# Transposing q and k on TensorE in place of DMA transposes, in an attention kernel with a gated MLP behind it

## Chip, cores and metric

The kernel runs on one core of a Trainium2 chip. The metric is the device time of one execution in microseconds; the time before is the median of 3 runs.

## What is computed

Eight batch entries, twelve heads, 448 positions, head dimension 64. q and k are normalised by their root mean square and scaled by g_q and g_k; then softmax attention; the heads are joined to rows of 768, and each entry goes through a gated MLP with a spatial mixing matrix.

```python
q_n, k_n = (rmsnorm(q, g_q), rmsnorm(k, g_k))        # x / sqrt(mean(x*x) + 1e-6) * g
scores = scale * np.matmul(q_n, k_n.transpose(0, 1, 3, 2))
attn = softmax(scores)
x = np.matmul(attn, v)  # heads joined: (8, 448, 768)
...
h = np.maximum(x @ w_in, 0.0)                        # w_in: 768 x 1024
u, v = h[..., :512], h[..., 512:]
v_n = (v - mu) / np.sqrt(var + 1e-06)
v_s = np.einsum('ts,bsd->btd', w_spatial, v_n) + b_spatial[None, :, None]
out = (u * v_s) @ w_out                              # w_out: 512 x 768
```

## The kernel before

**Tiling.** Positions lie as 112 partitions x 4 chunks (p c). The twelve heads of an entry are taken in three groups G of four heads (heads g, g+3, g+6, g+9); eight entries make 24 groups. Inside a group the heads form two pairs pr; a pair's two heads lie on the two halves of 128 partitions after a transpose. A *step* t is one score tile: one pair and two of the four chunks of keys, so a group is four steps, n = t % 4, and there are 96 steps and three more that drain.

**A group's way.** load (L70, SP's queue) brings q and k as float32. squares (L148, POOL) and reduce (L155, DVE) give the sums of squares; rstd (L162 and L163, ACT) gives 1/rms as Exp(-0.5 Ln); scaled (L168, POOL) multiplies into the bf16 tiles n0 and n1. Then q and k are turned so that the head dimension lies on partitions: for group 0 by transposes (L185, eight TensorE transposes into one PSUM buffer for a pair, evicted by DVE in L190 and L191, k with the gains g2_col), for all other groups by transpose_dma (L197, two DMA transposes on SP's queue, k into the tile kr) and k_scale (L205, DVE, from kr to kT). scores (L217) makes four matmuls of 64 x 112 by 64 x 448 into the PSUM tile pss (four banks), expo (L228, ACT) takes the exponential to bf16. Of the group before, sums (L238) adds the exponentials up, recip (L246 and L247, ACT) takes the reciprocal, values (L257) multiplies with v, and xt_store (L265, DVE) writes the product to xt.

**The MLP of an entry** is cut in units that fill PE between score tiles: unit_v (L283) with its relu (L275 on DVE, L273 on ACT), stats, ln_rstd and ln_apply (L289 to L303) for the LayerNorm, unit_u (L312), unit_s (L322) with the gating product (L325, DVE), and unit_o (L336) with its eviction (L341 on DVE, L339 on ACT) and the store (L345, SP's queue). s = (t - 15) % 12 says which units a step has: 0 to 2 unit_v, 3 to 5 unit_u, 6 and 7 unit_s, 8 to 11 unit_o. The units of an entry start four steps after its last score tile, so they run beside the next entry's scores; the last entry's run alone at the end.

**The order.** The scheduling is manual: each engine executes its instructions in the order in which the program's loop issues them. Within a step that order is: scores and expo, loads, the preparation of later groups (squares of group G+3 at n = 2 and 3; reduce at n = 3 and 0; rstd, scaled and transpose_dma of group G+2 at n = 1; k_scale of group G+1 at n = 0), the LayerNorm pieces, sums or values of group G-1, and then the MLP units. For groups 0 to 2 (t < 12) scores and expo go in halves of two matmuls and half an exponential, and groups 1 and 2 have preparation steps of their own at t = 0 to 6.

**Buffers.** All PSUM tiles other than pss come from one ring of four banks (ps_w), each taken again four allocations later: transposes, sums, values and all MLP units share it. n0 and n1 have two buffers each, qT, kT and kr three, the raw q and k tiles four.

```python
        if n == 1 and 3 <= T < NGT:      # T = G + 2
            rstd(T)
            scaled(T, 0)
            scaled(T, 1)
            transpose_dma(T, 0)
            transpose_dma(T, 1)
        if n == 0 and 3 <= K < NGT:      # K = G + 1
            k_scale(K)
```

Of the kernel before, what the change touches and what calls it, by code (L numbers as in the profile page):

```python
# [10 lines left out]
BF = mybir.dt.bfloat16  # L11
AF = mybir.ActivationFunctionType
ALU = mybir.AluOpType
# [5 lines left out]
def kernel(  # L19
# [17 lines left out]
    P = 112  # L37
    NC = 4
# [3 lines left out]
    pe, act, dve, pool, sync = nc.tensor, nc.scalar, nc.vector, nc.gpsimd, nc.sync  # L42
# [9 lines left out]
    qt_pool = ctx.enter_context(tc.tile_pool(name="qt", bufs=3))  # L52
# [13 lines left out]
    def load(G, i, l0=0, nl=4):  # L66
        b, g = divmod(G, NG)
        if (G, i) not in raw:
            raw[G, i] = qk_pool.tile([P, 4, NC * D], FP, name="qf" if i == 0 else "kf")
        sync.dma_start(out=raw[G, i][:, l0:l0 + nl], in_=(q_g, k_g)[i][b][g][:, l0:l0 + nl])  # L70

    def load_v(b):
        t = v_pool.tile([P, H, NC, D], BF, name="vt")
        pool.dma_start(  # L74
            out=t.rearrange("p h c d -> p h (c d)"),
            in_=v[b].rearrange("h (p c) d -> p h (c d)", c=NC))
        vb[b] = t
# [29 lines left out]
    for t in vn_t:  # L107
# [4 lines left out]
    g2_col = const.tile([128, 1], FP)  # L112
    dve.scalar_tensor_tensor(out=g2_row, in0=g_row[:, 0].rearrange("o t d -> o (t d)"), scalar=scale,
                             in1=g_row[:, 1].rearrange("o t d -> o (t d)"),
                             op0=ALU.mult, op1=ALU.mult)
# [3 lines left out]
    def load_w_in():  # L119
        for l in range(4):  # L120
            pool.dma_start(  # L121
                out=w_in[32 * l:32 * l + 32, :, :],
                in_=moe_w_in[192 * l:192 * l + 192, :].rearrange("(j p) f -> p j f", p=32))
# [16 lines left out]
    sqt, sqs, rst, nrm, qkt = {}, {}, {}, {}, {}  # L140
# [34 lines left out]
    def qk_tiles(G):  # L175
        if G not in qkt:
            qkt[G] = (qt_pool.tile([128, NC, 2, P], BF, name="qT"),
                      qt_pool.tile([128, NC, 2, P], BF, name="kT"))
        return qkt[G]

    def transposes(G, pr):
        ps = ps_w.tile([128, 8, 128], BF, name="ps")
        for i in range(2):
            for c in range(NC):
                pe.matmul(out=ps[:, 4 * i + c, 0:P],  # L185
                          lhsT=nrm[G, i][:, c, 2 * pr:2 * pr + 2, :],
                          rhs=ident[0:P, 0:P], is_transpose=True,
                          start=(i == 0 and c == 0), stop=(i == 1 and c == NC - 1))
        qT, kT = qk_tiles(G)
        dve.tensor_copy(out=qT[:, :, pr, :], in_=ps[:, 0:4, 0:P])  # L190
        dve.tensor_scalar(out=kT[:, :, pr, :], in0=ps[:, 4:8, 0:P], scalar1=g2_col, scalar2=None,  # L191
                          op0=ALU.mult)

    def transpose_dma(G, i):
        kr = qt_pool.tile([128, NC, 2, P], BF, name="kr") if i == 1 else None
        t = qk_tiles(G)[0] if i == 0 else kr
        sync.dma_start_transpose(out=t.rearrange("q c r p -> q (c r) p"),  # L197
                                 in_=nrm[G, i].rearrange("p c l d -> p (c l d)"))
        if i == 1:
            krs[G] = kr  # L200

    krs = {}

    def k_scale(G):
        dve.tensor_scalar(out=qkt[G][1], in0=krs.pop(G), scalar1=g2_col, scalar2=None, op0=ALU.mult)  # L205


    exps, xts = {}, {}
# [2 lines left out]
    def scores(t, half=None):  # L211
        G, n = divmod(t, 4)
        pr, c0 = n // 2, 2 * (n % 2)
        qT, kT = qkt[G]
        for c in (0, 1) if half is None else (half,):
            for h in range(2):
                pe.matmul(out=pss[:, 2 * c + h, 0:S],  # L217
                          lhsT=kT[64 * h:64 * h + 64, c0 + c, pr, :],
                          rhs=qT[64 * h:64 * h + 64, :, pr, :],
                          start=True, stop=True)  # L220

    def expo(t, half=None):
        G, n = divmod(t, 4)
        pr, c0 = n // 2, 2 * (n % 2)
        if c0 == 0 and half in (None, 0):
            exps[G, pr] = e_pool.tile([P, NC * 2, S], BF, name="et")
        a, m = (0, 4) if half is None else (2 * half, 2)
        act.activation(out=exps[G, pr][:, 2 * c0 + a:2 * c0 + a + m, :], in_=pss[:, a:a + m, 0:S],  # L228
                       func=AF.Exp, bias=0.0, scale=1.0)
# [118 lines left out]
    NGT = B * NG  # L348
    NST = NGT * 4
    for pr in range(2):  # L350
        l = 2 * pr
# [22 lines left out]
    for t in range(NST + 3):  # L374
        G, n = divmod(t, 4)
        s = t - 15
        b, s = divmod(s, 12)
        moe = b >= 0 and b < B - 1
        early = G < NG


        if t < NST:
            if early:
                if t > 0:
                    scores(t, 1)
                    expo(t, 0)
                expo(t, 1)
                if t + 1 < NST:
                    scores(t + 1, 0)
            else:  # L390
                if t == 12:
                    scores(t, 1)
                    expo(t, 0)
                    expo(t, 1)
                else:
                    scores(t)
                    expo(t)


        if G + 4 < NGT and n < 2:  # L400
            load(G + 4, n)
        if n == 1 and G % NG == 0 and G // NG + 1 < B:
            load_v(G // NG + 1)
        if t == 1:
            load_w_in()
        if t == 4:
            load_w_rest()


        if t == 0:  # L410
            rstd(1)
            scaled(1, 0)
            scaled(1, 1, eng=dve)
            squares(2, 0)
        elif t == 1:
            transpose_dma(1, 0)
            transpose_dma(1, 1)
            squares(2, 1, eng=dve)
            reduce(2, 0)
            reduce(2, 1)  # L420
        elif t == 2:
            k_scale(1)
            rstd(2)
            scaled(2, 0)
        elif t == 3:
            scaled(2, 1, eng=dve)
        if t == 4:
            transpose_dma(2, 0)
            transpose_dma(2, 1)
        if t == 6:  # L430
            k_scale(2)
        A, R, T, K = G + 3, G + 2, G + 2, G + 1
        if n == 2 and A < NGT:
            squares(A, 0)
        if n == 3 and A < NGT:
            squares(A, 1)
            reduce(A, 0)
        if n == 0 and 3 <= R < NGT:
            reduce(R, 1)
        if n == 1 and 3 <= T < NGT:  # L440
            rstd(T)
            scaled(T, 0)
            scaled(T, 1)
            transpose_dma(T, 0)
            transpose_dma(T, 1)
        if n == 0 and 3 <= K < NGT:
            k_scale(K)


        if moe:  # L450
            if s == 1:
                stats(b, 0)
            elif s == 2:
                stats(b, 1)
            elif s == 3:
                stats(b, 2)
                stats(b, 3)
                ln_rstd(b)
            elif s == 4:
                ln_apply(b)  # L460


        if 0 < G <= NGT:
            if n == 0:
                sums(G - 1)
                recip(G - 1)
            elif n < 3:
                values(G - 1, n - 1)
                xt_store(G - 1, n - 1)
        if t == 15:  # L470
            dve.tensor_copy(out=w_spT[96:113, NC - 1, :, :],
                            in_=bst[96:113, :].rearrange("q (p c) -> q c p", c=NC))
        if 15 <= t < 19:
            w_sp_unit(t - 15)


        if moe:
            if s == 0:
                unit_v(b, 0, dve)
                unit_v(b, 1, dve)  # L480
            elif s == 1:
                unit_v(b, 2, dve)
            elif s == 2:
                unit_v(b, 3, dve)
            elif s == 3:
                unit_u(b, 0, act)
            elif s == 4:
                unit_u(b, 1, act)
                unit_u(b, 2, act)
            elif s == 5:  # L490
                unit_u(b, 3, dve)
            elif s == 6:
                unit_s(b, 0)
                unit_s(b, 1)
            elif s == 7:
                unit_s(b, 2)
                unit_s(b, 3)
            elif s == 8:
                unit_o(b, 0, dve)
                unit_o(b, 1, act)  # L500
                unit_o(b, 2, dve)
            elif s == 9:
                unit_o(b, 3, dve)
                unit_o(b, 4, dve)
            elif s == 10:
                unit_o(b, 5, dve)
                unit_o(b, 6, act)
            else:
                unit_o(b, 7, dve)
# [44 lines left out]
```

## Time and profile before

| what | value |
|---|---|
| median of 3 runs | 354.74 us (354.63 to 356.36) |
| the profiled execution's own time | 354.63 us |
| its span, first to last instruction | 352.8 us |
| mean granted TensorE clock | 0.991 |
| busy: PE, ACT, DVE, POOL | 288.7, 222.0, 210.6, 186.3 us |
| DMA transposes, median from issue to landing | 2.9 us (q), 3.6 us (k), 23 each |
| SP's queue waiting with a transpose for POOL's n (L197) | 132.0 us |
| packets of the hardware DMA queue q1 | 69216, 43.59 MB |

How to read it: the span and the busy times are of one profiled execution, whose time is 1.8 us over its span. PE is TensorE's matmuls, PEld its weight loads, DVE, ACT, POOL and SP the vector, scalar, GpSimd and sync engines; L185 is line 185 of the kernel before. Matmuls are pipelined, and their records overlap: four score matmuls whose record lasts 0.58 us let the next matmul start after 0.52 us. In an answer on groups, "x23 | 11.7, 507 | 18.0 <-DMA kr<-n 18.0" is the count, busy microseconds, mean nanoseconds of one, and the idle microseconds before them with what ended them. In an answer on waits the three numbers are microseconds in all, times, and the longest. A timeline row is start, duration, engine, line and operation, with the idle time before it in brackets.

### The profile page before, as it was taken

To read this page: it belongs to the slowest core of one execution; us is meant where nothing else is said; L and a number is where in the kernel's file an instruction comes from. 1 tells how busy PE (TensorE), PEld (TensorE's weight loads), DVE (VectorE), ACT (ScalarE), POOL (GpSimd) and SP (SyncE) were. 2 spreads that over 40 slices of the span, in tenths; PEclk is the share of its full clock that TensorE was granted. 3 is DMA by queue.
4 is the path that set the end of the run, shared out by engine and by line. 5 is a ranking of instruction groups with operands and counts; after the bars stand their busy time and mean duration, and the time that the engine had idled before them with its cause. 6 is when DMAs were issued, how large, how long until landed. Compare 5 with 4: busy or idle time off the path is not lost.

```text
span 352.8 us, 5856 instructions
## 1 busy us (share of the span) xinstructions
PE 288.7 (82%) x2338; PEld 134.5 (38%) x2338; DVE 210.6 (60%) x352; ACT 222.0 (63%) x273; POOL 186.3 (53%) x113
## 2 busy tenths in 40 slices
PE   0222634688999989997999989998999899999993
PEld 0111201224435433542344434443444345445552
DVE  3385304226887587757764886488648865745551
ACT  2334434375778768874876786778677867785331
POOL 7259850926746774687197549654965484000000
PEclk9999999999999999998999999999999999999998
DMA  7979999497346994899339983999299554302305
GB/s 194 245 159 167 203 187 203 89 148 156 55 110 144 209 243 106 145 213 248 101 82 215 242 170 69 220 252 166 58 223 261 62 54 111 99 2 62 96 0 158
DMA packets 81651, 52.26 MB, mean 148 GB/s; under 512 B 44271, under 2 KB 77264, under 8 KB 81624
## 3 DMA queue, kind: packets, MB, share of 16 engines
q1 hardware_dynamic: 69216, 43.59, 57.2%
q0 software_dynamic: 12400, 8.30, 16.6%
q8 instruction: 18, 0.29, 0.4%
q14 instruction: 9, 0.07, 0.1%
q10 hardware_dynamic: 8, 0.00, 0.0%
HBM read 38.58 MB, written 11.01 MB: 141 GB/s over the span
## 4 chain that ended last, share of the span: by engine, by line
issue 37%; POOL 34%; PE 18%; DMA 7%; ACT 1%; DVE 1%; ACTq 0%; POOLq 0%; DVEq 0%
POOL sqt L148 19%; POOL n L168 12%; PE ps L336 5%; DMA qT<-n 4%; PE ps L283 4%; PE ps L312 3%; PE pss L217 2%; PE ps L257 2%; PE ps L322 2%; POOL vt L74 2%; ACT et L228 1%; DMA out_dram<-osb 1%; DMA g_row<-in_g_k_dram 1%; PE ps L238 1%; POOL w_in L121 1%
## 5 line engine op out<-in xcount | busy, mean ns | idle before, releaser
L228 ACT ACTIVATE et<-pss 112x1792 bf16<-112x1792 f32 (+1 forms) x109 | 160.4, 1483 | 68.8 <-PE pss L217 67.9
L168 POOL TENSOR_TENSOR n<-qf,rs 112x1024 bf16<-112x1024 f32 (+1 forms) x25 | 48.5, 1939 | 111.3 <-ACT rs L163 109.4
L217 PE MATMUL pss<-qT,kT 64*112 64x448 bf16 x384 | 64.6, 408 | 39.9 <-ACT et L228 33.0
L155 DVE TENSOR_REDUCE ms<-sqt 112x16 f32<-112x1024 f32 (+1 forms) x50 | 58.1, 1171 | 40.4 <-POOL sqt L148 38.4
L265 DVE TENSOR_TENSOR xt<-ps,rc 128x448 bf16<-128x448 f32 x48 | 29.6, 617 | 41.2 <-PE ps L257 35.7
L217 PEld LDWEIGHTS <-kT 64*112 64x112 bf16 x384 | 22.1, 134 | 79.2 <-issue 66.8
L257 PE MATMUL ps<-et,vt 112*32 112x448 bf16 x768 | 49.6, 382 | 0.0
L336 PE MATMUL ps<-w_out,gt 128*112 128x384 bf16 x256 | 47.5, 330 | 1.7 <-DVE osb L341 1.4
L283 PE MATMUL ps<-w_in,xt 128*112 128x512 bf16 x192 | 45.8, 383 | 0.1
L148 POOL TENSOR_TENSOR sqt<-qf 112x1024 f32<-112x1024 f32 x23 | 44.4, 1932 | 0.0
L312 PE MATMUL ps<-xt,w_in 128*128 128x448 bf16 x192 | 41.3, 361 | 2.2 <-DVE vs L275 2.2
L168 POOL TENSOR_TENSOR n<-kf,rs 112x1024 bf16<-112x1024 f32 x21 | 40.0, 1906 | 0.0
L148 POOL TENSOR_TENSOR sqt<-kf 112x1024 f32<-112x1024 f32 x21 | 39.7, 1890 | 0.0
L336 PEld LDWEIGHTS <-gt 128*112 128x112 bf16 x256 | 31.3, 129 | 18.4 <-issue 11.1
L283 PEld LDWEIGHTS <-xt 128*112 128x112 bf16 x192 | 23.4, 130 | 19.4 <-issue 6.6
L341 DVE COPY osb<-ps 112x384 f32<-112x384 f32 x46 | 24.4, 553 | 7.5 <-PE ps L336 5.9
L322 PE MATMUL ps<-w_spT,vn 112*128 112x448 bf16 (+1 forms) x128 | 26.9, 353 | 0.0
L257 PEld LDWEIGHTS <-vt 112*32 112x32 bf16 x768 | 16.8, 100 | 26.4 <-issue 19.5
L312 PEld LDWEIGHTS <-w_in 128*128 128x128 bf16 x192 | 17.6, 100 | 24.2 <-issue 11.1
L238 PE MATMUL ps<-et,ones 112*32 112x448 bf16 x384 | 24.8, 382 | 0.0
L325 DVE TENSOR_TENSOR gt<-ps,us 128x448 bf16<-128x448 f32 x32 | 20.0, 625 | 6.8 <-PE ps L322 4.5
L289 DVE BATCH_NORM_STATS2 s<-vs 112x6 f32<-112x512 bf16 x32 | 21.8, 680 | 2.5 <-ACT vs L273 2.5
(47 smaller groups left out, 184.0 us busy)
## 6 DMA issues: line engine op xcount, KB each, us to landing
out_dram<-osb SPq DMA_DIRECT2D x31, 336.0 KB, 3.6
qf<-in_q_dram SPq DMA_DIRECT2D x23, 448.0 KB, 6.3
kf<-in_k_dram SPq DMA_DIRECT2D x23, 448.0 KB, 7.4
vt<-in_v_dram POOLq DMA_DIRECT2D x8, 672.0 KB, 13.0
w_in<-in_moe_w_in_dram POOLq DMA_DIRECT2D x4, 384.0 KB, 11.9
w_out<-in_moe_w_out_dram POOLq DMA_DIRECT2D x1, 768.0 KB, 13.7
qf<-in_q_dram SPq DMA_DIRECT2D x2, 224.0 KB, 3.6
kf<-in_k_dram SPq DMA_DIRECT2D x2, 224.0 KB, 3.8
```

What stands on the lines that cost most here:

```text
L148: (eng or pool).tensor_tensor(out=t[:, 0:nl, :], in0=x, in1=x, op=ALU.mult)
L155: dve.tensor_reduce(out=sqs[G][:, i, NC * l0:NC * (l0 + nl)], in_=sqt.pop((G, i, l0))[:, 0:nl, :].rearrange("p l (c d) -> p (l c) d", d=D) ...
L168: (eng or pool).tensor_tensor(out=nrm[G, i][:, :, l0:l0 + nl, :].rearrange("p c l d -> p l c d"), in0=raw[G, i][:, l0:l0 + nl, :].rearrang ...
L217: pe.matmul(out=pss[:, 2 * c + h, 0:S], lhsT=kT[64 * h:64 * h + 64, c0 + c, pr, :], rhs=qT[64 * h:64 * h + 64, :, pr, :], start=True, stop ...
L228: act.activation(out=exps[G, pr][:, 2 * c0 + a:2 * c0 + a + m, :], in_=pss[:, a:a + m, 0:S], func=AF.Exp, bias=0.0, scale=1.0)
L238: pe.matmul(out=ps[32 * l:32 * l + 32, 0:S], lhsT=ones, rhs=exps[G, l // 2][:, 2 * c + l % 2, :], start=(c == 0), stop=(c == NC - 1), tile ...
L257: pe.matmul(out=ps[32 * l:32 * l + 32, 0:S], lhsT=vb[b][:, 3 * l + g, c, 32 * half:32 * half + 32], rhs=exps[G, l // 2][:, 2 * c + l % 2, ...
L265: dve.tensor_tensor(out=xts[b][:, 2 * g + half, :], in0=pst.pop((G, half))[:, 0:S], in1=rec[G], op=ALU.mult)
L283: pe.matmul(out=ps[0:P, :], lhsT=xts[b][:, j, c * P:(c + 1) * P], rhs=w_in[:, j, DH:DF], start=(j == 0), stop=(j == 5))
L312: pe.matmul(out=ps[:, 0:S], lhsT=w_in[:, j, 128 * f:128 * f + 128], rhs=xts[b][:, j, :], start=(j == 0), stop=(j == 5))
L322: pe.matmul(out=ps[:, 0:S], lhsT=vn_t[b % 2][0:kp, c, 128 * f:128 * f + 128], rhs=w_spT[0:kp, c, :, :].rearrange("p c s -> p (c s)"), star ...
L336: pe.matmul(out=ps[0:P, 0:384], lhsT=gts[b][:, f, c * P:(c + 1) * P], rhs=w_out[:, f, r], start=(f == 0), stop=(f == 3))
```

## The change

The change was announced as "every engine's order written out by hand in steps of four score tiles, one exponential per step, filler assigned to fixed steps". What the diff holds is one thing: transpose_dma and k_scale are removed, and groups 1 to 23 use the helper transposes, as group 0 does already. The scores, the exponentials (halves for t < 12, whole ones after), sums, values and MLP units keep their places.

For groups from 3 on, the call for a group's first pair of heads stands at n = 3, two steps after its scaled, and the one for the second pair at n = 0 of the next group; both stand after the step's scores and expo and ahead of sums or values and the MLP units in program order, on PE's and on DVE's queue alike. Each call takes one of the four PSUM buffers. The tile kr goes.

```diff
-    def transpose_dma(G, i):
-        kr = qt_pool.tile([128, NC, 2, P], BF, name="kr") if i == 1 else None
-        t = qk_tiles(G)[0] if i == 0 else kr
-        sync.dma_start_transpose(out=t.rearrange("q c r p -> q (c r) p"),
-                                 in_=nrm[G, i].rearrange("p c l d -> p (c l d)"))
-        if i == 1:
-            krs[G] = kr
-
-    krs = {}
-
-    def k_scale(G):
-        dve.tensor_scalar(out=qkt[G][1], in0=krs.pop(G), scalar1=g2_col, scalar2=None, op0=ALU.mult)
...
         elif t == 1:
-            transpose_dma(1, 0)
-            transpose_dma(1, 1)
+            transposes(1, 0)
             squares(2, 1, eng=dve)
             reduce(2, 0)
             reduce(2, 1)
         elif t == 2:
-            k_scale(1)
+            transposes(1, 1)
             rstd(2)
             scaled(2, 0)
         elif t == 3:
             scaled(2, 1, eng=dve)
         if t == 4:
-            transpose_dma(2, 0)
-            transpose_dma(2, 1)
+            transposes(2, 0)
         if t == 6:
-            k_scale(2)
+            transposes(2, 1)
...
             scaled(T, 0)
             scaled(T, 1)
-            transpose_dma(T, 0)
-            transpose_dma(T, 1)
-        if n == 0 and 3 <= K < NGT:
-            k_scale(K)
+        if n in (0, 3) and 3 <= G + (2 if n == 3 else 1) < NGT:
+            transposes(G + (2 if n == 3 else 1), 0 if n == 3 else 1)
```

## Prediction

> **What bounds the kernel now.** I read the engine shares first, then a table of busy time by stretches, then the waits inside the steady part, then the timeline of one group. A step is one score tile, four steps are one group of four heads, twelve steps are one batch entry; n is the step's place in its group, s its place in the entry's gated MLP.
>
> ```profile
> PE 288.7 (82%) x2338; PEld 134.5 (38%) x2338; DVE 210.6 (60%) x352; ACT 222.0 (63%) x273; POOL 186.3 (53%) x113
> ...
> PE   0222634688999989997999989998999899999993
> ```
>
> PE leads, but the slices show two regimes: up to about slice 9 (some 80 us) it is mostly idle, then full. The stretch from 79.5 us, where the first MLP units are issued, to 322.5 us:
>
> ```profile
> 79.50:322.50 243.00, 231.36 (x1956) 107.78 (x1959) 167.13 (x285) 179.16 (x205) 140.67 (x78) 0.99 0.73 146
> ```
>
> The columns are PE, weight loads, DVE, ACT, POOL. PE is busy for 231.4 of 243 us, the next engine (ACT) for 179. PE's waits in that stretch are few:
>
> ```profile
> PE pss L217 <- ACT et L228: 6.6, 5, 1.7
> PE ps L312 <- DVE vs L275: 2.2, 1, 2.2
> PE ps L336 <- DVE osb L341: 1.4, 6, 0.2
> ```
>
> So in the steady part whatever is added to PE's queue lengthens the run, except for what fills those 10 us. The page's chain of waits is not used: it runs through POOL and "issue" because POOL idles for its turn, and it does not show that PE has no gaps.
>
> Before 80 us, ACT's exponentials and PE's score matmuls take turns, and one stall is due to the transfers that the change removes (start, duration, what ended the idle time):
>
> ```profile
> 48.85 1.72 ACT L228 ACTIVATE et<-pss 112x896 bf16<-112x896 f32 x2 [2.88 <-PE pss L217]
> ...
> 53.57 0.45 DVE L205 TENSOR_SCALAR kT<-kr,g_col 128x896 bf16<-128x896 bf16 x1 [9.17 <-DMA kr<-n]
> ...
> 54.08 1.00 PE L217 MATMUL pss<-qT,kT 64*112 64x448 bf16 x4 [5.27 <-DVE kT L205]
> ...
> 55.11 1.72 ACT L228 ACTIVATE et<-pss 112x896 bf16<-112x896 f32 x2 [4.54 <-PE pss L217]
> ```
>
> The exponentials of steps 7 and 8 start 6.26 us apart. Step 11 has the same work in its order, and the one after it starts 2.80 us later (69.43 to 72.23). The stall is 3.5 us.
>
> **What the Trainium skill says.** "TensorE: Matmul & The Clock Gate", Part 4, PE-mode transpose: about 275 ns for one transpose in a kernel, and its output lands in PSUM, so that a copy is needed; this trace has 298 ns for each of group 0's transposes, and copies behind them. It adds that a transpose does not count as work for the clock gate; I therefore leave the early part at half clock (16 sums or values take 1.69 us there and 0.94 later). Same page, Back-to-back issue gap: a stream of load and matmul pairs runs at about 81 ns each at 128 columns, an isolated gap is columns/2.4 + 2.5 ns; no row of before shows either at full clock. "VectorE: DVE Perf Modes", Why PSUM operands drop a tier: a PSUM source loses the fastest copy mode; the trace agrees, 448 elements from PSUM take 0.39 to 0.44 us and 896 from SBUF take 0.51.
>
> ```profile
> L205 DVE TENSOR_SCALAR kT<-kr,g_col 128x896 bf16<-128x896 bf16 x23 | 11.7, 507 | 18.0 <-DMA kr<-n 18.0
> ...
> L185 PE MATMUL ps<-ident,n 112*128 112x112 bf16 x16 | 1.9, 298 | 8.5 <-POOL n L168 8.5
> ...
> L191 DVE TENSOR_SCALAR kT<-ps,g_col 128x448 bf16<-128x448 bf16 x2 | 0.9, 442 | 0.0
> ...
> L190 DVE COPY qT<-ps 128x448 bf16<-128x448 bf16 x2 | 0.8, 392 | 3.9 <-PE ps L185 3.9
> ```
>
> **Removed.** 46 DMA transposes (SP, L197) and 23 k_scale (DVE, 0.51 us). The transposes' landing (2.9 and 3.6 us median) lies three steps ahead of its use, so in the steady part it costs nothing, and removing it gains nothing. SP no longer waits for n (132 us of its waits); loads and stores behind it may start earlier, but no PE wait in the steady part names a load, so I price that at 0. The early stall goes: -3.5.
>
> **Added.** 46 calls of the transposes helper, 8 transposes and two DVE evictions each. How long PE is held by one call T: at half clock the eight in group 0 start 0.09 us apart, hence 0.75 us. At full clock nothing shows it. Lower end 8 x (112/2.4+2.5) = 0.4 us. Upper end: four transposes of w_sp hold PE for 0.53 us (89.05 to 89.58), 0.10 apart, hence 0.9 us for eight; but their weights are strided and load in 199 ns each, while contiguous 128-column loads (w_in, vn) take 97 to 100. I take the page's 81 ns scaled by 112/128, 8 x 71 = **0.57 us**; the sums, 16 pairs in 0.87 us, show that PE can issue at 54 ns.
>
> **Call at n = 3 (first half of group G+2): a new wait.** It stands behind that step's scores and ahead of all MLP filler; PE is in order, so the MLP units and the next scores behind it wait too, and through them ACT's exponentials; on DVE the evictions wait for it with LayerNorm statistics, relus and output copies behind them. It needs both n tiles, which rest on a chain that begins with the scores of n = 1: exponential, Ln and Exp of rstd, two POOL multiplications.
>
> ```profile
> 220.51 0.59 PE L217 MATMUL pss<-qT,kT 64*112 64x448 bf16 x4
> ...
> 223.10 0.23 ACT L163 ACTIVATE rs<-lnms 112x32 f32<-112x32 f32 x1
> ...
> 223.41 1.90 POOL L168 TENSOR_TENSOR n<-qf,rs 112x1024 bf16<-112x1024 f32 x1 [3.29 <-ACT rs L163]
> ...
> 225.27 1.90 POOL L168 TENSOR_TENSOR n<-kf,rs 112x1024 bf16<-112x1024 f32 x1
> ...
> 225.68 0.58 PE L217 MATMUL pss<-qT,kT 64*112 64x448 bf16 x4
> ```
>
> From 220.51 to 227.17 is 6.66 us, and 6.66 to 6.70 in the other groups. PE reaches the call two steps and one score tile later: 5.17+0.52 = 5.69 us for s = 10 to 0; 5.44+0.52 = 5.96 for s = 2 to 4; 6.02+0.52 = 6.54 for s = 6 to 8. With 0.08 us for the semaphore PE would wait 1.05, 0.78 and 0.20 us. The four q transposes fit in that wait, so the call costs the wait plus 0.29 for k, or 0.57 if that is more: 1.34, 1.07, 0.57. There are 19 such calls after 79.5 us (groups 5 to 23): 7x1.34 + 6x1.07 + 6x0.57 = **19.2 us**.
>
> **Call at n = 0 (second half):** its n is long ready: 19x0.57 = **10.8 us**.
>
> **DVE and the four PSUM buffers.** A call's two evictions take 0.74 us (10.40 to 11.14), so DVE gains 2x0.74-0.5 = 1.0 us per group of 11.8, at 69% busy: no bound. But at n = 3 the evictions stand behind reduce(G+3, q), which waits for POOL:
>
> ```profile
> 217.38 1.22 DVE L155 TENSOR_REDUCE ms<-sqt 112x16 f32<-112x1024 f32 x1 [1.83 <-POOL sqt L148]
> ```
>
> That ends 9.8 us after the scores of n = 1 (208.80), the evictions 10.5 after. At s = 8 three unit_o take the other three buffers, PE is through them and the next scores at 6.54+0.57+2.09+0.52 = 9.7, and the n = 0 call needs the first buffer: 0.8 us of waiting, less the 0.24 before unit_o that it replaces: 6x0.6 = **3.6 us** (0 to 5). At s = 0 and 4 another buffer is free.
>
> **Given back.** PE waits for the exponential at s = 5 because ACT is held by the LayerNorm statistics (6.6 us in all). PE will reach that point over 1 us later: **-6 us** (0 to -6.6).
>
> **The early steps.** Six calls (steps 4, 6, 7, 8, 11, 12) fall between a score tile and the next in the turn-taking with ACT: 6x0.75 = 4.5 us. The two of steps 1 and 2 put DVE's evictions ahead of squares(2, k), whose reduce releases rstd(2) and the exponential of step 3: about +1. With the stall gone: 4.5+1-3.5 = **+2 us** (-1 to +5; a clock that rises earlier would take some of it back).
>
> **Sum.** 19.2+10.8+3.6-6+2 = +29.6 us on the profiled execution's 354.63 us (span 352.8, 1.8 around it); that stands 0.1 under the median of 354.74. So **384.3 us**.
>
> **Rivals.**
> - *Only the instruction time counts* (0.20). If the n = 3 wait is hidden, because steps n = 1 and 2 lengthen for another reason: 38x0.57-6+2 = +17.7, 372 us. Against it: the chain and PE's way to it both start at the same scores, and no call lies between.
> - *Dear transposes* (0.20). At 0.9 us a call: 19x0.9 at n = 0; at n = 3 the same waits plus 0.45, 7x1.5+6x1.23+6x0.9; +2, -6, +2: 38 us more, 393 us; queues on DVE could bring it to 400. For it: the w_sp row. Against it: the shorter loads.
> - *Faster* (0.04). The DMA relief decides: the early stall (3.5 us) and the wait at step 3 for kT (3.9 us) go, and transposes disappear in PE's remaining idle time, 347 us. It turns from the point where a call costs under (11.6+7.4)/46 = 0.41 us and no call waits for n. For it: 0.4 is the lower bound. Against it: the waits, and that PE's idle time lies at s = 5, not at the calls.
> - *Little net effect* (0.06). Cheap calls partly in idle time, and a quicker start: 353 to 366 us. That the change does nothing is excluded: the diff puts 368 matmuls in PE's queue.
>
> **How the numbers follow.** The main case has 0.50 and reaches from 378 (calls at 0.4 us, a quicker start) to 391. Going into the two slower-side rivals until 0.2 is left out gives 369 to 398. A measurement tells about 0.5% (1.8 us) from no change. Faster 0.04, same 0.02, slower 0.94.
>
> **What would show it.** PE's line for the transposes: 368 records, and a wait of PE for POOL's n of about 0.2 to 1 us in each group, some 13 us in all; a wait for DVE's eviction at the s = 9 calls; the waits for the exponential at s = 5 gone; the entry's twelve steps going from 35.5 to about 40 us; the exponential of step 13 about 2 us later. It is wrong if PE does not wait for n, if eight transposes hold PE outside 0.4 to 0.9 us, or if POOL's chain gets shorter.

## The result

| | before | changed |
|---|---|---|
| median of 4 runs | 355.55 us (354.63 to 358.85) | 375.23 us (374.77 to 375.90) |
| span of the profiled execution | 352.8 us | 373.6 us |

The ratio is 1.0537, with a 95% interval of 1.0464 to 1.0611: the change makes the kernel 5% slower. The forecast was 384.3 us with a range of 369 to 398. The direction and the mechanism held, the sum was 9 us too dear. The number alone does not decide for that mechanism: it lies under the main case, which reached down to 378 us, and nearer to the 372 us of the rival in which only instruction time counts. The waits below and e1 decide.

The page of the changed kernel, engine shares and PE's slices:

```profile
PE 311.9 (83%) x2706; PEld 152.9 (41%) x2706; DVE 226.8 (61%) x421; ACT 226.0 (61%) x273; POOL 185.4 (50%) x113
...
PE   0233666679999999999999999999999999999994
```

368 matmuls more on PE, which was the bound already, and its slices are now full from the tenth (84 us) to the last but one. The steady stretch, from the first score tile of step 15 to a little behind that of step 95 (PE, weight loads, DVE, ACT, POOL), has grown:

```profile
81.50:343.80 262.30, 248.25 (x2260) 121.13 (x2263) 180.42 (x342) 183.19 (x206) 141.11 (x79) 1.00 0.41 98
```

Between the scores of step 15 and of step 95 lie 259.5 us, where there were 240.3 before. PE's waits in this stretch, to be held against the three lines in the prediction (us in all, times, longest; the program lost 13 lines, so the scores are now L204):

```profile
PE ps L185 <- POOL n L168: 7.1, 12, 1.1
PE ps L185 <- DVE kT L191: 5.4, 6, 0.9
PE pss L204 <- ACT et L215: 0.9, 1, 0.9
```

All three waits of before are gone or nearly so, and the two that the prediction named have come. The list counts the wait for n only from the end of the q transposes, so it has 7.1 us where the prediction expected some 13; counted from PE's arrival, as the prediction did, it is 11.5 us in 12 calls, all at s = 0 and 4. The first of the two waits, at s = 0 (start, duration, what ended the idle time):

```profile
238.32 1.90 POOL L168 TENSOR_TENSOR n<-kf,rs 112x1024 bf16<-112x1024 f32 x1
...
238.72 0.59 PE L204 MATMUL pss<-qT,kT 64*112 64x448 bf16 x4
...
239.24 0.37 PE L185 MATMUL ps<-ident,n 112*128 112x112 bf16 x4
...
240.27 0.37 PE L185 MATMUL ps<-ident,n 112*128 112x112 bf16 x4 [0.67 <-POOL n L168]
...
240.48 2.76 PE L270 MATMUL ps<-w_in,xt 128*112 128x512 bf16 x12
```

The four q transposes go at once, the four of k stand until POOL is done with n at 240.22, and unit_v behind them stands as well: the call holds PE from 239.24 to 240.48, 1.24 us. The second, at s = 9:

```profile
228.81 1.22 DVE L155 TENSOR_REDUCE ms<-sqt 112x16 f32<-112x1024 f32 x1 [1.80 <-POOL sqt L148]
...
229.95 0.38 DVE L190 COPY qT<-ps 128x448 bf16<-128x448 bf16 x1
230.25 0.44 DVE L191 TENSOR_SCALAR kT<-ps,g_col 128x448 bf16<-128x448 bf16 x1
...
230.75 0.57 PE L185 MATMUL ps<-ident,n 112*128 112x112 bf16 x8 [0.91 <-DVE kT L191]
```

DVE's reduce waits for POOL, the evictions of the n = 3 call wait behind the reduce, and PE waits for the PSUM buffer that they free. A whole entry takes 38.8 us from score tile to score tile, where the prediction expected about 40.

### The profile page after: what moved, and what is told of

It is laid out like the page before. It is cut to its first block, busy times and chain, and to the rows that moved or that the text cites. A ratio compares the mean times of both kernels' runs of the same rounds, so it can differ in the third digit from the quotient of the medians.

```text
span 373.6 us, 6607 instructions
## 1 busy us (share of the span) xinstructions
PE 311.9 (83%) x2706; PEld 152.9 (41%) x2706; DVE 226.8 (61%) x421; ACT 226.0 (61%) x273; POOL 185.4 (50%) x113
## 4 chain that ended last, share of the span: by engine, by line
issue 38%; POOL 35%; PE 21%; DVE 3%; DMA 1%; POOLq 1%; ACTq 0%; DVEq 0%
POOL sqt L148 19%; POOL n L168 12%; PE ps L299 4%; PE ps L270 4%; PE ps L309 3%; PE ps L323 3%; PE ps L244 3%; PE pss L204 2%; PE ps L225 2%; POOL vt L74 2%; DVE ms L155 1%; DMA g_row<-in_g_k_dram 1%; POOL w_in L121 1%; POOLq L532 1%; DVE kT L191 0%
## 5 line engine op out<-in xcount | busy, mean ns | idle before, releaser
L204 PE MATMUL pss<-qT,kT 64*112 64x448 bf16 x384 | 64.4, 403 | 27.7 <-ACT et L215 26.2
L185 PE MATMUL ps<-ident,n 112*128 112x112 bf16 x384 | 32.9, 232 | 21.8 <-POOL n L168 16.3
L244 PE MATMUL ps<-et,vt 112*32 112x448 bf16 x768 | 48.8, 377 | 0.0
L204 PEld LDWEIGHTS <-kT 64*112 64x112 bf16 x384 | 21.1, 132 | 66.9 <-issue 64.8
L148 POOL TENSOR_TENSOR sqt<-qf 112x1024 f32<-112x1024 f32 x23 | 43.5, 1892 | 0.0
L299 PE MATMUL ps<-xt,w_in 128*128 128x448 bf16 x192 | 40.1, 353 | 0.0
L185 PEld LDWEIGHTS <-n 112*128 112x128 bf16 x384 | 22.7, 107 | 40.9 <-POOL n L168 20.2
L190 DVE COPY qT<-ps 128x448 bf16<-128x448 bf16 x48 | 18.4, 383 | 17.7 <-PE ps L185 17.7
L244 PEld LDWEIGHTS <-vt 112*32 112x32 bf16 x768 | 16.7, 99 | 25.6 <-issue 16.2
## 6 DMA issues: line engine op xcount, KB each, us to landing
vt<-in_v_dram POOLq DMA_DIRECT2D x8, 672.0 KB, 10.8
w_in<-in_moe_w_in_dram POOLq DMA_DIRECT2D x4, 384.0 KB, 11.5
```

The costliest lines, as they stand in the source:

```text
L148: (eng or pool).tensor_tensor(out=t[:, 0:nl, :], in0=x, in1=x, op=ALU.mult)
L185: pe.matmul(out=ps[:, 4 * i + c, 0:P], lhsT=nrm[G, i][:, c, 2 * pr:2 * pr + 2, :], rhs=ident[0:P, 0:P], is_transpose=True, start=(i == 0 a ...
L204: pe.matmul(out=pss[:, 2 * c + h, 0:S], lhsT=kT[64 * h:64 * h + 64, c0 + c, pr, :], rhs=qT[64 * h:64 * h + 64, :, pr, :], start=True, stop ...
L244: pe.matmul(out=ps[32 * l:32 * l + 32, 0:S], lhsT=vb[b][:, 3 * l + g, c, 32 * half:32 * half + 32], rhs=exps[G, l // 2][:, 2 * c + l % 2, ...
L299: pe.matmul(out=ps[:, 0:S], lhsT=w_in[:, j, 128 * f:128 * f + 128], rhs=xts[b][:, j, :], start=(j == 0), stop=(j == 5))
```

## The experiments

In the diffs, lines without a sign are context. The theory is the prediction's: PE pays for the calls, for the wait for n and for the buffer. The rival to it in e1 to e3 is the one that was put at 372 us, in which only instruction time counts. The kernels of a set ran beside runs of the kernel before, whose medians were 357.5 (e1 to e4), 354.5 (e5 to e7) and 355.3 us (e8, e9). Where medians of two sets are compared, the start times of score tiles in the traces are given too.

**e1: rstd ahead of the exponential.**

```diff
+        if n == 1 and not early and G + 2 < NGT:
+            rstd(G + 2)
         if t < NST:
...
         if n == 1 and 3 <= T < NGT:
-            rstd(T)
+            if early:
+                rstd(T)
             scaled(T, 0)
```

> The changed kernel with rstd of n = 1 issued on ACT ahead of that step's exponential instead of behind it (steps from 13 on), nothing else moved. Theory (PE waits at the n = 3 call for POOL's n, which hangs on that exponential and rstd): n is ready some 1.7 us earlier, the n = 3 calls at s = 0 and s = 4 fall from 1.25 and 0.97 us to about 0.45, so 7 x 0.8 + 6 x 0.5 = 8.7 us less: about 366.5 us, and PE's waits for n in the steady part gone. Rival (only the instructions of the calls cost, the wait hides other waiting): 374 to 376 us, with the wait coming back elsewhere on PE.

Measured: 360.34 us, ratio to before 1.0100 (1.0025 to 1.0176): 15 us under the changed kernel, where 8.7 were expected; from step 15 to step 95 its trace is 15.6 us shorter. PE's waits from 79.5 us on:

```profile
PE pss L204 <- ACT et L215: 1.8, 1, 1.8
PE ps L323 <- DVE gt L312: 0.3, 1, 0.3
```

Both new waits are gone, not the one alone. In the score tiles' start times an entry is 2.55 us shorter: 0.83 at s = 0, 0.56 at s = 4, 0.17 at s = 5, and 0.97 at s = 9, where PE had waited for its buffer. POOL's squares stand behind its scaled, so when n is ready earlier the reduce and the evictions behind it are earlier too. The gains stand at the two calls and at the buffer, and nowhere else, so it is not ACT's order in general that gained. The rival falls: the wait for n was not hidden.

**e2: the evictions ahead of the reduce.**

```diff
+        if n == 3 and 3 <= G + 2 < NGT:
+            transposes(G + 2, 0)
         if n == 2 and A < NGT:
             squares(A, 0)
         if n == 3 and A < NGT:
             squares(A, 1)
             reduce(A, 0)
...
-        if n in (0, 3) and 3 <= G + (2 if n == 3 else 1) < NGT:
-            transposes(G + (2 if n == 3 else 1), 0 if n == 3 else 1)
+        if n == 0 and 3 <= G + 1 < NGT:
+            transposes(G + 1, 1)
```

> The changed kernel with the n = 3 call issued ahead of squares and reduce of that step, so that on DVE its two evictions stand before the reduce that waits for POOL; PE's own order stays. Theory (at s = 9 PE waits for the PSUM buffer of the n = 3 call, 0.9 us in each of six entries, because the evictions stand behind that reduce): about 5.4 us less, of which up to 1.4 comes back as unit_o's wait for its eviction: 370 to 371.5 us. Rival (the buffer wait only stands in for a queue that DVE has anyhow): 374 to 376 us, the wait moving to sums or unit_o.

Measured: 368.13 us, ratio 1.0310 (1.0215 to 1.0405); 7.1 us less than the changed kernel. The wait for kT is gone from PE's list, the 7.1 us for n stay, and unit_o's wait did not come back. The time lies 1.9 us under the range expected (370 to 371.5). In the score tiles the gain is 0.98 us at s = 9 and 0.18 at s = 5 in each entry, 5.4 us from step 15 to step 95; the trace begins 0.6 us earlier at step 0, ahead of anything that was moved, and the rest of the 7.1 lies within the spread of the runs.

**e6: both moves.** The two diffs together.

> The changed kernel with both moves: rstd ahead of the exponential at n = 1, and the n = 3 call ahead of squares and reduce. Alone they took 15 and 7 us off. Theory (the wait for n and the buffer wait at s = 9 hang on the same POOL queue; with n 1.3 us earlier squares and the reduce are earlier too and the buffer wait has gone already): within 1 us of the first move alone, 359 to 361 us. Rival (two separate costs that add): 353 to 355 us.

Measured: 359.70 us, ratio 1.0156 (1.0098 to 1.0214), 0.6 under e1, which is within the spread of the runs. The savings do not add: the two waits hang on the same queue of POOL, and whichever move makes the evictions earlier takes the buffer wait away.

**e3: the matmuls of the n = 0 calls issued twice.**

```diff
-        for i in range(2):
+        for i in (0, 1) * times:
             for c in range(NC):
...
-            transposes(G + (2 if n == 3 else 1), 0 if n == 3 else 1)
+            transposes(G + (2 if n == 3 else 1), 0 if n == 3 else 1, 2 if n == 0 and G > 2 else 1)
```

> The changed kernel with the eight matmuls of each n = 0 call from group 3 on issued twice into the same buffer (21 calls, the output is the same). It prices a call on PE alone, with no new wait, eviction or buffer. Theory: 8 x 0.05 = 0.4 us each, with some in the wait for other engines: 375.2 + 7 to 9 = 382 to 384 us. Rival (PE's time is not what ends the run, the waits for n and for DVE are): under 377 us.

Measured: 381.74 us, ratio 1.0696 (1.0609 to 1.0783): 6.5 us more, 0.3 us short of the range expected and well over the rival's 377. (The condition doubles 20 calls, not 21.) In a typical entry the three doubled calls add 0.39 at s = 9, 0.39 at s = 1 and only 0.22 at s = 5, where sums already stood 0.10 us for a buffer.

**e9: the same on top of e1**, where hardly a wait is left.

> The kernel of e1 (no waits for n or for buffers left) with the eight matmuls of each n = 0 call from group 4 on issued twice into the same buffer (20 calls, the output is the same). Theory (with the waits gone the calls' own time is all that is left): 20 x 0.4 us = 8 us over e1's 360.3, 367 to 369.5 us. Rival (PE has idle time again once the waits are gone, and takes the extra work for nothing): 360 to 364 us.

Measured: 368.85 us, ratio 1.0372 (1.0317 to 1.0426): 8.5 us over e1 by the medians of two sets, 0.42 us for each of 20 calls. In the traces an entry is 1.18 us longer for its three calls, 0.39 us each. That is nearly all of the 0.41 us that eight transposes hold PE: in the steady part it has nothing to hide a call behind.

**e4: TensorE transposes for groups 1 and 2 alone** (the kernel before, with the changed kernel's edits at t = 1, 2, 4 and 6 only).

```diff
         elif t == 1:
-            transpose_dma(1, 0)
-            transpose_dma(1, 1)
+            transposes(1, 0)
...
         elif t == 2:
-            k_scale(1)
+            transposes(1, 1)
...
         if t == 4:
-            transpose_dma(2, 0)
-            transpose_dma(2, 1)
+            transposes(2, 0)
         if t == 6:
-            k_scale(2)
+            transposes(2, 1)
```

> The kernel before with TensorE transposes for groups 1 and 2 alone; from group 3 on the DMA transposes and k_scale stay. Theory (in the steady part DMA transposes cost nothing, and in the early part the transposes remove a stall of 3.5 us at step 8 for some 0.6 us a call): the changed kernel's scores of step 8 begin 1.2 us earlier than before although three calls and a late step 3 lie ahead; without group 3's call at step 7 that is about 2 us: 352 to 354 us against 354.7 before. Rival (early calls cost what they save, or the stall moves to group 3's DMA transposes): 354.5 to 357 us.

Measured: 355.97 us against 357.5 beside it, ratio 0.9948 (0.9900 to 0.9995). In the trace step 8 begins at 51.55 us instead of 54.08, so the early calls do gain there. How much of it reaches the end is less sure. By time it is about 2 us, and the interval only just leaves 1; as a number, 355.97 us lies in the rival's range, since the whole set ran slower. In the profiled execution the gain was lost again: PE's idle time between the scores of steps 15 and 95 is 16.2 us, against 11.6 before, and step 95 begins 2.0 us later than before.

**e5: k_scale two steps later, DMA transposes kept.** The prediction put PE's wait at s = 5 down to ACT, and its end to PE's later arrival. The trace before shows another candidate: SP's transpose, the DVE row that needs it, and the idle time before it (s = 1, in five entries 1.0 to 2.4 us):

```profile
227.19 3.67 SPq L197 DMA_TRANSPOSE kr<-n  x1
...
233.80 0.45 DVE L205 TENSOR_SCALAR kT<-kr,g_col 128x896 bf16<-128x896 bf16 x1 [1.21 <-DMA kr<-n]
```

This transpose lands 6.6 us after its issue, the median one after 3.6: v's 672 KB were put in POOL's queue at 219.14 and landed at 232.1. In the steady part all five k transposes that were issued with a v load under way took 6.0 to 7.6 us to land, the others 2.9 to 4.5. That the load is the reason was not tested. DVE stands with the LayerNorm statistics queued behind k_scale. ACT's wait for them, over the steady part of before:

```profile
ACT lv L297 <- DVE mv L290: 15.0, 7, 4.9
```

and of the changed kernel:

```profile
ACT lv L284 <- DVE mv L277: 2.2, 7, 0.4
```

```diff
-        if n == 0 and 3 <= K < NGT:
+        if n == (0 if early else 2) and 3 <= K < NGT:
             k_scale(K)
```

> The kernel before with k_scale from group 4 on moved from n = 0 to n = 2 (still two steps ahead of its use), DMA transposes kept. In the trace before, k_scale waits on DVE once per entry for a late DMA transpose of k (1.0 to 2.4 us, always after a v load), ahead of the LayerNorm statistics of s = 1. Theory (that wait holds DVE, then ACT's ln_rstd, then PE at s = 5 for 1.5 to 1.7 us and once 2.2 us; so these waits were a hidden cost of the DMA transposes): PE's waits of 6.6 + 2.2 us go, 346 to 349 us against 354.7, as in the changed kernel. Rival (as in the prediction: the wait at s = 5 comes from the order of ACT and goes only when PE arrives later): 353.5 to 356 us, the s = 5 waits still there.

Measured: 349.27 us, ratio 0.9867 (0.9826 to 0.9908); the saving is 5.3 us, 0.3 us short of the range expected. From 79.5 us on, PE's waits and ACT's for the statistics:

```profile
PE pss L217 <- ACT et L228: 4.3, 5, 0.9
PE ps L336 <- DVE osb L341: 2.3, 6, 0.4
...
ACT lv L297 <- DVE mv L290: 10.7, 8, 1.6
```

The 2.2 us at unit_u are gone; at s = 5 0.86 us stay, where four of the five waits were 1.5 to 1.7. Each side had a part: k_scale's place makes 4.5 us of these waits of PE (2.2 and 6.6 less 4.3, with shorter ones), the other 4.3 stay. Moved were both k_scale's wait and its own 0.5 us on DVE; the run does not part them.

The saving in time is not all of this. From step 15 to step 95 the trace is 4.8 us shorter. PE's waits together make 2.8 of it, as those for unit_o and w_spT grew by 1.7 us; about 1.7 us are a stretch of lower granted clock that the trace before has and this one has not (see "Left over" below). So some 3 us are shown to come from the waits.

**e7: e4 and e5 together.**

> The kernel before with TensorE transposes for groups 1 and 2 alone and DMA transposes with k_scale at n = 2 for group 4 and later. Theory (two separate savings, 2.5 us at step 8 and 8 to 9 us from k_scale's wait): 343 to 347 us, under both kernels. Rival (the savings are of the same waiting, or the DMA transposes go late by more): 348 to 353 us.

Measured: 348.15 us, ratio 0.9832 (0.9786 to 0.9879), faster than both kernels. Against e5 beside it that is 1.1 us, so of e4's gain about half is left, and the range expected was missed by 1 us. The traces differ by 1.06 us at step 15 already and by 0.3 in the steady part; e5's own trace had reached step 12, where its edit begins, 0.45 us earlier than the one before, so a part of what is missing is the spread of the starts.

**e8: what is left at s = 5.**

```diff
             elif s == 3:
                 stats(b, 2)
                 stats(b, 3)
-                ln_rstd(b)
             elif s == 4:
+                ln_rstd(b)
                 ln_apply(b)
```

> The kernel of e7 with ln_rstd issued at s = 4 behind that step's exponential instead of at s = 3 ahead of it. Theory (what is left of PE's wait at s = 5, 0.9 us in each of five entries, comes from ACT's order: ln_rstd waits for the last LayerNorm statistics of DVE with the exponential queued behind it): these waits go, 4 us less, 343 to 345 us. Rival (DVE itself is late, and the wait moves to unit_s, which needs the applied LayerNorm): 347 to 349 us.

Measured: 342.32 us, ratio 0.9638 (0.9605 to 0.9671), the fastest. PE's list from 79.5 us on no longer has the exponential:

```profile
PE ps L336 <- DVE osb L341: 2.1, 6, 0.3
PE ps L133 <- DVE w_spT L137: 0.8, 1, 0.8
PE ps L336 <- DVE gt L325: 0.3, 1, 0.3
```

The rest of the s = 5 wait was ACT's order: the exponential stood behind an ln_rstd that waited for DVE. It saved 5.8 us by the medians of two sets, where 4 were expected, and 4.9 us between steps 15 and 95 of the traces.

## Why the prediction was right, and where its sum was off

The terms, from the start times of score tiles and of calls in the two traces:

| term | predicted, us | measured, us |
|---|---|---|
| 19 calls at n = 3, with their wait for n | 19.2 | 16.8 |
| 19 calls at n = 0 | 10.8 | 10.8 |
| buffer wait at s = 9, less unit_o's | 3.6 | 4.0 (6 x 0.90 - 1.4) |
| PE's waits given back | -6 | -9.6 (6.6 at s = 5, 2.2 at unit_u, 0.7 for w_spT) |
| steps up to 15 | +2 | +2.1 |
| left over | 0 | -3 |
| sum | 29.6 | 21 (score tile of step 95: 21.2 later) |

**The bound.** Right. PE had no room: e9 charges 0.39 us for eight more transposes, where eight hold PE for 0.41.

**The wait for n.** Right, to 0.03 us: q's start to k's start is 1.03 us at s = 0 and 0.75 at s = 4, where 1.05 and 0.78 were worked out. At s = 8 POOL is done 0.13 us after PE has come to the call (226.93 and 226.80), and the q transposes cover it, as the prediction had it for its 0.20. e1 shows that it hangs on ACT's exponential and rstd.

**The price of one call.** Mis-sized: 0.57 us predicted. At s = 8, with nothing to wait for, the eight hold PE from 265.61 to 266.02, **0.41 us**, or 0.05 each; k's half is 0.21, not 0.29. That is the lower end of the prediction's bounds, columns/2.4 + 2.5 ns (49 ns for 112). The 81 ns of the Trainium skill ("TensorE: Matmul & The Clock Gate", Back-to-back issue gap), scaled to 71, were the wrong choice here: the page has them as the sustained figure for pairs of a load and a matmul and says that the formula under-counts there, but these eight pairs take 51 ns each. The transposes in this trace (ns least, median, most):

```profile
L185 PE MATMUL ps<-ident,n x384: 212/213/301, 10.0 to 321.6; 112*128 112x112 bf16 x192
```

The 301 ns belong to the early pace of PE, which the prediction calls half clock (16 sums or values take 1.69 us), the 213 to the later pace, its full clock (0.94 us). At s = 0, 4 and 8 together this makes the 2.4 us of the first row. The second row came out right by two errors, which is luck: most calls at s = 1 and 9 hold PE for 0.50 us, but those at s = 5 for 0.67 and the first, at step 16, for 0.96, because sums behind them waits for its PSUM buffer, where the prediction said that another buffer was free.

**"Removing it gains nothing" in the steady part.** This step failed. The prediction took the median landing (3.6 us) against three steps of slack, and that no PE wait named a transfer. But in five entries k's transpose is late, k_scale stands, and the wait passes through DVE and ACT before it reaches PE, where the list shows the exponential. e5 takes 4.5 us of PE's waits away by k_scale's place alone. So the term "given back" was right in sign and too small. Its stated reason, that PE arrives later, can hold only for the other 4.3 us at s = 5, and is not shown for them: e8 removes them by ACT's order, in a kernel where PE does not arrive later.

**The buffer.** Right in place and size (0.90 us against 0.8), shown by e2.

**The early steps.** Right in size: step 8 begins 1.2 us earlier in the changed kernel, step 15 2.1 us later. But 0.6 us of that lateness stands at step 0 already, ahead of the first instruction that differs, so the change's own part is 1.5. PE keeps its early pace there: the eight hold it for 0.86 us (48.00 to 48.86), 0.1 more than worked out.

**Left over.** Between 154.5 and 190 us the trace before has a granted clock of 0.95 (0.53 from 165.5 to 169.1), the changed one 1.00. The entry there takes 38.2 us before, where its neighbours take 35.6; 2.2 of the difference are the wait at unit_u and it had 1.3 less of the wait at s = 5, so about 1.7 us fall to the clock. It makes the difference between the two traces smaller than the change's own price. Over 1 us stays unexplained.

**The faster rival** put its turning point at 0.41 us a call and no wait for n. A call with nothing to wait for and a unit behind it takes just that, but the wait for n came. e1 has no such wait, its 38 calls hold PE for 0.46 us on average, and it lands 1% above the kernel before. One reading of this rival was wrong, the 3.9 us at step 3:

```profile
31.64 0.16 PEld L217 LDWEIGHTS <-kT 64*112 64x112 bf16 x1 [3.92 <-DVE kT L205]
...
33.51 0.99 PE L217 MATMUL pss<-qT,kT 64*112 64x448 bf16 x4 [5.05 <-ACT et L228]
```

It is a weight load that waits for kT there; the matmul behind it waits longer, for ACT's exponential.

## What to carry to other kernels

Before putting work on an in-order engine that has no gaps, follow its inputs back to a common start and compare the two ways in time: here both began at the same score tile, and the chain through ACT and POOL was up to 1.05 us longer than PE's own way. A wait in a list names the last engine in a row of waits: look one and two engines further back before you say that a transfer costs nothing. And the place of short instructions in the order of an engine with idle time mattered here: moving rstd took 15 us off the changed kernel, moving k_scale and ln_rstd 3 to 5 and 5 to 6 us off kernels with DMA transposes, beside the 20 us that the change itself cost.

## What the runs showed of the hardware

Eight TensorE transposes of 112 columns with contiguous 128-column weights hold PE for 0.41 us at its later pace (16 sums in 0.94 us) and 0.86 at the early one (1.69 us). The four of a w_sp unit, whose 112 weight columns lie four elements apart, start 0.10 to 0.14 us apart at the later pace (89.05 to 89.40), and their loads take 199 ns, against 98 for the 128 contiguous columns; which of the two differences costs it was not tested. In the steady part a DMA transpose of k that was issued while 672 KB of v were loading landed after 6.0 to 7.6 us, otherwise after 2.9 to 4.5 us.
